# Another order of all steps up to the attention's end, in attention followed by two MLPs

## The chip, the cores and the metric

The kernel runs on one core of a Trainium2 chip. The metric is the device time of one launch in microseconds (us), and less is better. The kernel before took 616.63 us (median of 3 runs, 615.5 to 617.96).

## The reference

All inputs and outputs are float32. The attention takes `q`, `k`, `v` of shape (2, 8, 768, 64): 2 batches, 8 heads, 768 positions, 64 numbers per head. Each position attends to the positions less than 16 away and to 24 block summaries (the maximum of the keys, the mean of the values over 32 positions):

```python
k_sum = k.reshape(B, H, nb, block, D).max(axis=3)     # block = 32
v_sum = v.reshape(B, H, nb, block, D).mean(axis=3)
scores_l = scale * np.matmul(q, k.transpose(0, 1, 3, 2))   # masked outside the window
scores_s = scale * np.einsum('bhsd,bhnd->bhsn', q, k_sum) + np.log(block)
a = softmax(np.concatenate([scores_l, scores_s], axis=-1))
x = np.matmul(a, np.concatenate([v, v_sum], axis=2))       # then to 1536 tokens x 512
h = x @ w_in;  x = (h * (1 / (1 + np.exp(-h)))) @ w_out    # first MLP: 512 -> 2048 -> 512
out = ((x @ w_a) * (x @ w_b)) @ w_out2                     # second: 512 -> 1536 -> 512
```

## The kernel before

TensorE multiplies in a reduced float32 format (fp32r). To keep the precision, each operand of a large product is split into a high part, rounded to fp32r, and a low part, the rest; a product is then three matmuls (high by high, high by low, low by high).

The work has three stages. The first does the attention and, woven into it, the first MLP for tokens 0 to 895 or so; the second finishes the first MLP; the third is the second MLP. The change touches the first stage alone.

The attention goes in 24 steps, 12 per batch, each for 64 positions of all 8 heads. Ahead of a batch's steps the keys are brought into place and transposed on TensorE (`tk`), copied into window tiles (`wk`), and their block maxima taken (`mk`, joined by `sk`, put into the windows by `pk`); the values are loaded (`LG`), summed (`sv`), averaged by matmuls (`mv`) and kept (`kv`, copied on by the DMAs `PV`); the queries are transposed (`tq`) and scaled (`bq`). A step `n` then goes through scores (`sc`, TensorE, L403), masking with the row maximum (`sm`, VectorE, L427 or L433), exp (`ex`, ScalarE, L447), the sums (`rs`), the scaling (`no`, L462), a transpose (`tr`, TensorE, L468) and its copy out of PSUM (`pc`), the product with the values (`av`, TensorE, L483), and the split of the result into the high and low parts of the MLP's input x (`xh`, `xl`, L497).

The first MLP works on blocks of 512 tokens (8 attention steps) and pieces of 128 of the 2048 hidden units. For slot `i` (block `i // 16`, piece `i % 16`), `m1` makes the h tile with 12 matmuls (L579), `sg` applies Silu, `gh` and `gl` split it, and `m2` adds its share to the four y banks with 12 matmuls (L612). `m1` needs the piece of `w_in`, `m2` that of `w_out`, both loaded (`LI`, `LO`), decoded from raw words (`da` on ScalarE, `du` and `dj` on VectorE, L523, L529 and L533) and split (`hi`, `lo`, L556). A decoded `w_out` piece is also spilled to DRAM (`SP`) and read again for the later blocks (`RO`, `hR`, `lR`). The key, query, value and weight loads are all issued from SP's queue. Steps named `dm` with the letter y run four transposes on TensorE that keep it busy; with n they do nothing.

The order of all of this is one text, `ORDER` (L28 to L79): 797 words, carried out from left to right. Each word names a step, the numbers say which tile, and the last letter says which engine a movable step uses: `a` ScalarE, `v` VectorE, `p` GpSimd; for `sc` and `av` the last letter says whether a step opens new PSUM banks (n) or takes the second halves of those of the step before it (s). Each engine, and SP's queue, works through its own instructions in the order of the text, and an instruction that waits holds back everything behind it on its engine. Buffers are shared in small rings (four tiles of raw weight words, three decoded ones, three split `w_out` pieces, three g tiles, two h banks, four tiles of scores), and the next user of a ring waits for the release. After the last word a loop runs slots 28 to 47 with a fixed pattern, `m1` of a slot and then `m2` of the slot two before.

```python
        for word in ORDER.split():
            name, *a = word.split(":")
            ops[name](*(int(x) if x.isdigit() else x for x in a))
```

Of the kernel before, what the change touches and what calls it, by code (L numbers as in the profile page):

```python
# [32 lines left out]
sc:0:n sm:0 dm:8:n ex:1 rs:1 no:2:v LI:1 mv:0:1:0:1 mv:0:3:0:4 sv:0:2:1:p mv:0:2:0:1 kv:0:0:v LI:2 no:1:p ex:3 rs:3 ex:0 qz
tq:0:1:0 tq:0:1:1 bq:0:1:1:v tr:1 LV:1 pc:1:v du:in:2 du:in:1 dm:2:y bq:0:1:0:a sc:4:n sm:4 da:in:2 no:3:p da:in:1 tr:3
sc:5:n rs:0 no:0:p dj:in:2 sc:7:s dm:3:n tr:2 PV:0:1 LV:3 ex:4 av:1:n sm:7 PV:0:3 rs:4 LQ:0:2 tr:0 sm:5 hi:in:2:p pk:0:2:p
pc:3:a ex:7 xh:1:v pc:0:v av:3:n xh:3:v pc:2:a xl:1 LV:0 no:4:p sc:6:n lo:in:2:p dm:4:y rs:7 sm:6 xl:3 tq:0:2:0 no:7:p
tq:0:2:1 bq:0:2:1:v tr:4 ex:5 av:0:n xh:0:v ex:6 rs:6 dj:in:1 bq:0:2:0:a no:6:p PV:0:2 LV:2 av:2:n xh:2:a dm:9:n tr:7 xl:0
# [5 lines left out]
tr:8 pc:8:a tk:1:0:1 gh:2:a gl:2:p gh:0:a m1:4 mk:1:0:1 gl:0:v dj:in:7 hi:in:3:v lo:in:3:p tk:1:0:0 av:8:n LV:11 av:11:s
gh:1:a wk:1:0:1:a mk:1:0:0 LK:1:2 tk:1:2:1 wk:1:1:1:a hi:in:7:a xh:8:v xh:11:v tk:1:2:0 LQ:1:0 tq:1:0:0 tq:1:0:1 mk:1:2:1
wk:1:2:0:v mk:1:2:0 LI:6 sk:1:v wk:1:0:0:a tr:10 LO:1 gl:1:p xl:8 wk:1:2:1:a pk:1:0:v LV:9 lo:in:7:p xl:11 du:out:1 m1:3 tr:9
bq:1:0:1:a bq:1:0:0:a sc:15:n sc:13:s da:in:6 pc:10:a du:in:6 sg:3:p dj:in:6 sc:14:n sc:12:s da:out:1 dj:out:1 hi:in:6:a
lo:in:6:p LV:10 pc:9:a sm:15 hi:out:1:a lo:out:1:p sm:12 LO:0 LI:13 da:in:13 sm:13 av:10:n LI:5 SP:1 du:in:13 sg:4:p dj:in:13
av:9:s da:out:0 hi:in:13:a xh:9:a du:out:0 du:in:5 xh:10:a dj:out:0 sm:14 m1:6 sg:6:v xl:9 lo:in:13:p hi:out:0:a lo:out:0:v
da:in:5 LO:2 du:out:2 dj:in:5 da:out:2 dj:out:2 hi:in:5:v m1:7 boot LG:1:0 su:15:v LG:1:1 m2:0 ex:12 LQ:1:1 gh:6:v lo:in:5:v
m2:1 xl:10 hi:out:2:v lo:out:2:v gl:6:v LO:3 LI:8 da:out:3 du:out:3 SP:0 rs:12 dj:out:3 hi:out:3:v LG:1:2 tq:1:1:0 LG:1:3  # L50
tq:1:1:1 bq:1:1:0:a gh:3:a ex:14 SP:3 m2:2 da:in:8 bq:1:1:1:a gl:3:v sv:1:1:1:p sg:7:p lo:out:3:v m1:5 m2:3 no:12:v LO:5
sv:1:2:1:v mv:1:2:256:1 sv:1:0:1:v mv:1:0:256:1 pk:1:1:p mv:1:1:0:1 sv:1:3:1:v mv:1:3:0:1 LO:4 sg:5:v gh:5:a du:in:8 rs:14
no:14:p ex:15 kv:1:2:a gl:5:v LI:10 du:out:4 kv:1:0:a pk:1:2:a SP:2 dj:in:8 da:out:4 dj:out:4 LV:14 LV:12 hi:in:8:a lo:in:8:v
m1:13 hi:out:4:a tr:14 pc:14:a LI:9 lo:out:4:p gh:4:a du:out:5 tr:12 pc:12:v da:out:5 dj:out:5 hi:out:5:a su:13:v ex:13 m1:8
gl:4:v LO:7 rs:13 sc:18:n sc:16:s du:in:9 sm:16 sm:18 da:in:9 SP:4 LO:6 da:out:6 du:out:6 dj:in:9 PV:1:2 no:13:p rs:15 ex:18
m2:4 dj:out:6 LV:15 tr:13 LO:8 av:14:n av:12:s xh:12:v lo:out:5:p m2:5 sg:13:p xl:12 SP:5 xh:14:v hi:in:9:p LO:10 lo:in:9:p
no:15:v du:in:10 m1:9 pc:13:a LV:13 da:in:10 tr:15 du:out:8 hi:out:6:a lo:out:6:p xl:14 m2:6 sg:8:v gh:8:v da:out:8 gl:8:v
sg:9:v PV:1:3 SP:6 dj:in:10 du:out:7 gh:9:a PV:1:1 dj:out:8 pc:15:a hi:in:10:v da:out:7 dj:out:7 av:15:n LI:11 lo:in:10:v
av:13:n du:out:10 gh:7:a xh:13:v xl:13 xh:15:a xl:15 gl:9:v hi:out:7:a hi:out:8:v LI:15 lo:out:7:p m1:10 lo:out:8:v sc:17:n
gl:7:v sc:19:s LQ:1:2 du:in:11 sm:17 SP:8 m2:7 m2:8 ex:16 su:17:p LI:12 da:in:11 dj:in:11 hi:in:11:v sm:19 rs:16 SP:7  # L60
tq:1:2:1 ex:17 da:out:10 LO:9 tq:1:2:0 m1:16 du:in:12 da:in:12 dj:in:12 rs:17 no:17:v lo:in:11:p LI:14 sg:10:v hi:in:12:v
gh:10:a gl:10:v bq:1:2:0:a LV:18 du:out:9 da:out:9 lo:in:12:v bq:1:2:1:a dj:out:9 LO:11 m1:12 dj:out:10 hi:out:9:a SP:10
lo:out:9:p m2:9 da:in:14 rs:18 no:18:p du:in:14 dj:in:14 hi:in:14:v hi:out:10:a lo:out:10:v tr:18 lo:in:14:p LO:13 sg:16:p
du:out:11 LO:12 du:out:12 SP:9 da:out:11 dj:out:11 SP:11 tr:17 da:out:12 dj:out:12 m1:11 SP:12 sg:12:v LO:14 gh:12:v gl:12:v
sg:11:v gh:11:v m2:10 hi:out:11:a lo:out:11:p gl:11:v da:in:15 pc:18:v gh:13:v gl:13:p m1:22 da:out:13 m2:11 du:in:15
dj:in:15 LV:17 pc:17:v hi:out:12:p LV:16 no:16:v lo:out:12:v tr:16 av:17:n gh:16:a m1:14 du:out:14 LO:15 du:out:15 hi:in:15:p
sg:22:p lo:in:15:p da:out:14 m2:12 gl:16:v m1:17 dj:out:14 SP:14 hi:out:14:v da:out:15 dj:out:15 ex:19 du:out:13 dj:out:13
first xh:17:v SP:13 pc:16:v hi:out:13:v lo:out:13:v xl:17 sc:22:n sc:21:s sm:21 sg:14:p m2:13 gh:14:v gl:14:p m1:15 sm:22
sc:20:n lo:out:14:p m2:14 su:21:v sm:20 rs:19 ex:21 sg:15:v sg:17:p no:19:v su:22:p ex:22 tr:19 av:18:n gh:15:v hi:out:15:v
RO:18 lo:out:15:v LV:19 SP:15 gh:17:a av:16:s xh:18:a m1:18 rs:22 ex:20 rs:21 no:21:v RO:17 hR:17:a gl:15:v xh:16:a m2:15  # L70
yh:0:2 xl:18 xl:16 RO:16 yh:0:1 pc:19:v yh:0:0 sc:23:n hR:16:v lR:16:v yh:0:3 gl:17:p sm:23 m1:19 hR:18:p RO:25 lR:18:p
sg:18:p tr:21 gh:18:p gl:18:v m2:16 lR:17:p m2:17 m2:18 sg:19:p m1:21 RO:23 hR:23:v no:22:v LV:21 rs:20 no:20:v gh:19:p
gl:19:p m1:24 gh:22:v gl:22:p sg:21:p gh:21:p gl:21:v RO:19 lR:23:v tr:20 pc:21:a av:21:n av:19:s xh:19:a pc:20:a hR:19:v
sg:24:p ex:23 LV:23 rs:23 m1:20 sg:20:p xl:19 xh:21:a xl:21 RO:21 lR:19:p m2:19 gh:20:p RO:20 gl:20:v hR:20:v m1:25 m1:23
sg:23:p tr:22 lR:20:v m2:20 hR:21:p RO:27 hR:27:p lR:21:v m2:21 lR:27:p m1:27 gh:24:a gl:24:v RO:22 hR:22:a gh:23:v gl:23:v
RO:24 lR:22:p m2:22 no:23:p pc:22:v hR:24:p lR:24:p LV:22 m2:23 m2:24 tr:23 sg:25:v hR:25:v gh:25:v av:22:n gl:25:v m1:26
# [1083 lines left out]
```

## Time and profile before

| | |
|---|---|
| median of 3 runs | 616.63 us |
| the profiled execution | 617.56 us |
| its span, first to last instruction | 615.9 us |
| TensorE busy | 605.8 us of the span |
| VectorE, ScalarE, GpSimd busy | 397.7, 281.2, 279.3 us |
| TensorE's mean granted clock | 0.992 of full speed |

In the rows PE is TensorE's matmuls, PEld its weight loads, DVE VectorE, ACT ScalarE, POOL GpSimd, and SPq SP's queue; "L612" is a line of the kernel. The granted clock is given as a share of 2.4 GHz. Busy times of PE overlap from one matmul to the next, so a stop is seen from the starts and from the brackets, which give the idle time before an instruction and what ended it.

### The profile page before, as it was taken

To read this page: it belongs to the slowest core of one execution; us is meant where nothing else is said; L and a number is where in the kernel's file an instruction comes from. 1 tells how busy PE (TensorE), PEld (TensorE's weight loads), DVE (VectorE), ACT (ScalarE), POOL (GpSimd) and SP (SyncE) were. 2 spreads that over 40 slices of the span, in tenths; PEclk is the share of its full clock that TensorE was granted. 3 is DMA by queue.
4 is the path that set the end of the run, shared out by engine and by line. 5 is a ranking of instruction groups with operands and counts; after the bars stand their busy time and mean duration, and the time that the engine had idled before them with its cause. 6 is when DMAs were issued, how large, how long until landed. Compare 5 with 4: busy or idle time off the path is not lost.

```text
span 615.9 us, 10100 instructions
## 1 busy us (share of the span) xinstructions
PE 605.8 (98%) x3650; PEld 529.8 (86%) x3650; DVE 397.7 (65%) x778; ACT 281.2 (46%) x615; POOL 279.3 (45%) x269
## 2 busy tenths in 40 slices
...
PEclk9699999999999999999999999999999999999999
...
GB/s 222 191 240 232 252 315 227 259 232 105 44 56 79 78 86 218 221 227 173 200 192 171 48 52 147 128 208 135 144 186 96 195 35 87 82 219 315 120 0 137
DMA packets 90522, 97.82 MB, mean 159 GB/s; under 512 B 39000, under 2 KB 68440, under 8 KB 90472
## 3 DMA queue, kind: packets, MB, share of 16 engines
...
## 4 chain that ended last, share of the span: by engine, by line
PE 93%; DVE 3%; DMA 2%; issue 1%; ACT 0%; SPq 0%; DVEq 0%; ACTq 0%
PE y L612 21%; PE h L579 21%; PE bankg L823 14%; PE bankh L823 14%; PE ol L870 11%; PE o L849 5%; PE av L483 2%; PE sc L403 2%; PE pt L468 2%; DMA st_in<-in_moe_w_in_dram 1%; DMA st_k<-in_k_dram 1%; PE vsum L340 1%; PE qt L264 1%; PE kt L264 1%; DVE ks L302 1%
## 5 line engine op out<-in xcount | busy, mean ns | idle before, releaser
L612 PE MATMUL y<-g,w_out 128*128 128x512 f32 x576 | 139.1, 392 | 1.2 <-DVE st L433 1.0
L579 PE MATMUL h<-x,w_in 128*128 128x512 f32 (+1 forms) x600 | 139.9, 384 | 0.0
L612 PEld LDWEIGHTS y<-g,w_out 128*128 128x128 f32 x576 | 107.0, 188 | 25.3 <-ACT w_out L151 1.4
L579 PEld LDWEIGHTS h<-x,w_in 128*128 128x128 f32 x600 | 108.4, 188 | 21.8 <-DVE w_in L556 0.2
L556 POOL TENSOR_TENSOR w_out<-re_out,w_out 128x512 fp32r<-128x512 f32 x39 | 54.7, 1404 | 99.4 <-ACT w_out L151 95.0
L870 PE MATMUL ol<-w_out,plh 128*128 128x512 f32 x192 | 59.0, 389 | 0.0
L594 DVE TENSOR_TENSOR g<-h,g 128x512 fp32r<-128x512 f32 x31 | 21.4, 690 | 37.2 <-ACT g L151 36.9
L587 ACT ACTIVATE h<-h 128x512 f32<-128x512 f32 x31 | 18.2, 586 | 56.6 <-PE h L579 56.5
L556 POOL TENSOR_TENSOR w_out<-w_out,w_out 128x512 fp32r<-128x512 f32 x20 | 28.4, 1428 | 33.7 <-ACT w_out L151 26.4
L788 POOL TENSOR_TENSOR ab<-sum,ab 128x384 f32<-128x384 f32 x24 | 27.3, 1144 | 33.7 <-DVE sum L785 33.7
L870 PEld LDWEIGHTS ol<-w_out,plh 128*128 128x128 f32 x192 | 36.0, 188 | 7.5
L870 PE MATMUL ol<-w_out,pll 128*128 128x512 f32 x96 | 37.3, 389 | 0.0
L862 DVE TENSOR_TENSOR pll<-pl,plh 128x1024 fp32r<-128x1024 f32 x12 | 17.2, 1430 | 30.7 <-ACT plh L861 30.7
L151 ACT CAST w_out<-re_out 128x512 fp32r<-128x512 f32 x34 | 21.1, 621 | 27.9 <-issue 23.2
L849 PE MATMUL o<-w_out,p 128*128 128x512 f32 x108 | 28.5, 393 | 0.0
L823 PE MATMUL bankh<-yhT,wab 128*128 128x384 f32 x96 | 28.2, 334 | 0.0
L462 POOL TENSOR_TENSOR sm<-sm,st 128x480 f32<-128x480 f32 x14 | 15.3, 1095 | 27.6 <-DVE st L458 16.7
L533 DVE SCALAR_TENSOR_TENSOR w_out<-w_out,u_out 128x512 uint32<-128x512 uint32 x28 | 23.9, 860 | 4.2 <-ACT w_out L523 3.1
L766 ACT COPY sum<-bankh 128x384 f32<-128x384 f32 x12 | 5.7, 478 | 38.9 <-PE bankh L823 38.9
L594 POOL TENSOR_TENSOR g<-sg,g 128x512 fp32r<-128x512 f32 x8 | 10.7, 1343 | 27.8 <-ACT g L151 13.9
L523 ACT ACTIVATE w_out<-st_out 128x512 f32<-128x512 f32 x28 | 18.8, 674 | 9.5 <-DMA st_out<-in_moe_w_out_dram 5.1
L806 ACT CAST p<-ab 128x384 fp32r<-128x384 f32 x12 | 6.2, 514 | 35.5 <-POOL ab L788 18.0
...
## 6 DMA issues: line engine op xcount, KB each, us to landing
...
```

The source lines that it names most:

```text
L151: nc.scalar.copy(o, i)
L523: nc.scalar.activation(w32, stage_t[kind, f][:, :, 1].bitcast(F32), AF.Prelu, scale=2.0 ** -112, alpha=2.0 ** 32)
L533: nc.vector.scalar_tensor_tensor(bits, bits, 3, u_t.pop((kind, f)), op0=ALU.logical_shift_left, op1=ALU.bitwise_or)
L556: engine.tensor_tensor(w[:, 1], w32_t[kind, f], w[:, 0].bitcast(F32), op=ALU.subtract)
L579: nc.tensor.matmul(h_ps[i][:, cols], win_t[f][:, a, c * P:(c + 1) * P], x_t[n][:, steps, m, c, :], start=(idx == 0), stop=(idx == 3 * NK - 1))
L587: nc.scalar.activation(sg_t[i], ps, AF.Silu)
L594: engines[engine].tensor_tensor(g_t[i][:, 1], sg_t.pop(i), g_t[i][:, 0].bitcast(F32), op=ALU.subtract)
L612: nc.tensor.matmul(y_ps[n, c], wout_t[i][:, a, c * P:(c + 1) * P], g_t[i][:, m, :], start=(f == 0 and (a, m) == (0, 0)), stop=(f == N1 - 1 ...
L788: engines["v" if k == 6 else "p"].tensor_tensor(at, x, at, op=ALU.mult)
L823: nc.tensor.matmul((A, B)[b], weights(u, a, s, s + 1)[:, 0, c * P:(c + 1) * P], yc_t[q, y][m][:, c, :], start=(idx == 0 and not more), sto ...
L849: nc.tensor.matmul(o_ps[t], g[:, a, c:c + P], w[:, m], start=(begins and (a, m) == (0, 0)), stop=(ends and (a, m) == PARTS[-1]))
L870: nc.tensor.matmul(late_o[j], late_p[f][a][:, j * P:(j + 1) * P], wo2_t[N2 + f][:, m], start=(f == 0 and (a, m) == (0, 0)), stop=(f == N2 ...
```

## The change

The text of `ORDER` is replaced. The same 797 words stand in it, but in another order; for 132 of them the letter of the engine is another one, and 10 of the `sc` and `av` words and six `dm` words change their last letter (five `dm` words run in either order). No function of the kernel changes. The start of the two texts, to a little past the first `m1`:

```diff
-LKq:0:0 br:k:0:0:a dm:1:y tk:0:0:1 c2 LKq:0:2 ok:0 br:k:0:2:v tk:0:0:0 mk:0:0:0 tk:0:2:0 mk:0:2:0 wk:0:0:1:a c1 wk:0:0:0:a
-wk:0:2:0:a tk:0:2:1 LKq:0:1 br:k:0:1:v tk:0:1:1 tk:0:1:0 mk:0:2:1 dm:7:y LQq:0:0 dm:11:y wk:0:2:1:a mk:0:0:1 LG:0:1
-br:q:0:0:v tq:0:0:0 wk:0:1:0:a tq:0:0:1 mk:0:1:1 LG:0:0 mk:0:1:0 sk:0:v bq:0:0:0:a bq:0:0:1:a wk:0:1:1:v c3 pk:0:0:a sc:2:n
-sm:2 sc:1:n pk:0:1:a LG:0:2 sm:1 sv:0:1:1:p ex:2 sc:3:n sm:3 LG:0:3 LQ:0:1 rs:2 sv:0:3:4:v sv:0:0:4:p mv:0:0:512:4 dm:0:n
...
-sc:11:n sc:9:s dm:5:n LI:0 pc:4:a rs:5 hi:in:1:a no:5:p xl:2 pc:7:a sc:8:n ok:1 sc:10:s sm:11 tr:6 LV:7 sm:9 tr:5 LV:5 sm:10
-ex:11 av:7:n pc:6:a LV:4 av:4:n rs:11 xh:7:a xl:7 xh:4:a sm:8 dm:10:n pc:5:a lo:in:1:p LV:6 dm:6:n no:11:p m1:1:0 LK:1:1 ex:8
+c1 LKq:0:0 c3 dm:9:y LKq:0:1 br:k:0:1:a br:k:0:0:v tk:0:0:0 tk:0:0:1 ok:0 wk:0:0:1:a LKq:0:2 br:k:0:2:p mk:0:0:0 wk:0:0:0:a
+LQq:0:0 br:q:0:0:p tk:0:1:1 mk:0:1:1 wk:0:1:1:a qz LG:0:1 tk:0:1:0 wk:0:1:0:a mk:0:0:1 dm:4:n c2 tk:0:2:1 dm:11:y mk:0:2:1
+wk:0:2:1:a tk:0:2:0 mk:0:2:0 tq:0:0:0 bq:0:0:0:a mk:0:1:0 sk:0:v pk:0:0:p LG:0:3 wk:0:2:0:a tq:0:0:1 sv:0:3:4:p dm:10:y
+dm:5:n bq:0:0:1:v sc:2:n sm:2 ex:2 sc:1:n LG:0:0 sm:1 sv:0:1:1:p sc:3:n sm:3 ex:3 rs:2 no:2:v sv:0:0:4:p LQ:0:1 tq:0:1:0 rs:3
+ex:1 dm:6:y sc:0:s tq:0:1:1 dm:0:n sm:0 bq:0:1:1:v LG:0:2 sv:0:2:1:v pk:0:2:v bq:0:1:0:a mv:0:0:512:4 mv:0:1:0:1 mv:0:3:0:4
...
+xl:0 pc:7:v sc:11:n LI:0 da:in:0 sc:9:s sm:9 tr:6 LV:4 av:4:n sc:8:n sc:10:s LV:7 pc:6:a dm:8:n dm:3:n dm:1:y xh:4:v xl:4
+sm:11 ex:11 LV:6 av:6:s dj:in:2 sm:8 av:7:n LI:7 xh:7:a xl:7 tr:5 xh:6:v xl:6 hi:in:2:p m1:1:0 pc:5:a LV:5 av:5:s ex:9
+du:in:0 dj:in:0 rs:9 lo:in:2:p xh:5:a hi:in:0:p xl:5 sm:10 LK:1:0 tk:1:0:0 mk:1:0:0 ex:8 rs:8 su:10:v LI:4 da:in:4 ex:10
+LK:1:1 lo:in:0:p du:in:4 no:8:v dj:in:4 hi:in:4:p m1:2 sg:2:p LK:1:2 lo:in:4:p gh:2:a m1:1:1 sg:1:p gh:1:a tk:1:1:1 rs:10
...
```

## Rows read from the trace of the kernel before

**Rows 1.** The page's slices: TensorE's granted clock, in tenths of full speed, 40 slices.
```profile
PEclk9699999999999999999999999999999999999999
```

**Rows 2.** Stretches: busy us of each engine (instructions), granted clock, DMA share, GB/s.
```profile
6.30:16.40 10.10, 7.04 (x76) 5.73 (x76) 8.93 (x16) 7.36 (x25) 5.05 (x8) 1.00 1.12 249
16.50:26.70 10.20, 10.20 (x70) 9.38 (x70) 5.97 (x23) 6.94 (x33) 5.22 (x6) 0.50 0.80 183
26.80:40.40 13.60, 13.60 (x270) 11.38 (x268) 12.74 (x70) 11.43 (x48) 9.19 (x12) 1.00 1.01 209
40.40:72.30 31.90, 30.81 (x319) 26.82 (x316) 27.81 (x93) 26.95 (x70) 12.08 (x10) 1.00 1.03 260
72.30:223.20 150.90, 150.60 (x957) 122.05 (x958) 104.84 (x246) 78.55 (x162) 51.83 (x47) 1.00 0.53 151
```

**Rows 3.** The chain that ended last, in order of time: start us, us, what.
```profile
96.17 2.99 PE y L612 x12
...
329.33 8.16 PE y L612 x36
```

**Rows 4.** TensorE's timeline, 0 to 16 us: start, us, instruction, idle before it.
```profile
6.36 1.10 PE L264 MATMUL kt<-ident,raw_k 128*128 128x128 f32 x8 [0.40 <-ACT raw_k L151]
...
9.86 1.09 PE L264 MATMUL kt<-ident,raw_k 128*128 128x128 f32 x8 [0.95 <-DVE raw_k L153]
...
14.74 1.35 PE L403 MATMUL sc<-kin,qb 64*64 64x120 f32 x32 [1.60 <-ACT kin L151]
```

**Rows 5.** TensorE's timeline, 16 to 75 us.
```profile
20.86 2.92 PE L340 MATMUL vsum<-vg,sel 96*120 96x128 f32 x12
23.56 1.91 PE L264 MATMUL qt<-ident,raw_q 128*128 128x128 f32 x8
...
40.42 1.68 PE L579 MATMUL h<-x,w_in 128*128 128x256 f32 x12
...
65.62 5.75 PE L579 MATMUL h<-x,w_in 128*128 128x512 f32 x24
72.37 2.95 PE L612 MATMUL y<-g,w_out 128*128 128x512 f32 x10 [1.00 <-DVE st L433]
```

**Rows 6.** VectorE's timeline: copies of keys and queries, the joins, x.
```profile
7.07 0.69 DVE L153 COPY raw_k<-st_k 128x1024 f32<-128x1024 f32 x1 [3.90 <-DMA st_k<-in_k_dram]
...
11.00 0.69 DVE L153 COPY raw_q<-st_q 128x1024 f32<-128x1024 f32 x1
...
12.99 1.31 DVE L308 TENSOR_TENSOR ks<-ks 128x96 f32<-128x96 f32 x1
...
43.61 0.89 DVE L497 TENSOR_TENSOR x<-av,x 128x256 fp32r<-128x256 f32 x2 [0.29 <-ACT x L151]
...
59.93 0.26 DVE L308 TENSOR_TENSOR ks<-ks 128x96 f32<-128x96 f32 x1
```

**Rows 7.** ScalarE's timeline: the first copy, and the starts of two exps.
```profile
5.26 1.05 ACT L151 COPY raw_k<-st_k 128x1024 f32<-128x1024 f32 x1 [2.96 <-DMA st_k<-in_k_dram]
...
32.36 0.40 ACT L447 ACTIVATE sm<-sm,st 128x120 f32<-128x120 f32 x1
...
34.03 0.36 ACT L447 ACTIVATE sm<-sc,st 128x120 f32<-128x120 f32 x1
```

**Rows 8.** GpSimd's timeline: two copies.
```profile
30.25 0.61 POOL L153 CAST w_in<-w_in 128x512 fp32r<-128x512 f32 x1
30.80 0.34 POOL L153 COPY kin<-ks 128x192 f32<-128x192 f32 x1
```

**Rows 9.** Groups by shape, 0 to 224 us: count, busy us, mean ns, idle before.
```profile
L433 DVE CUSTOM_DVE_ANT_0 sm<-sc,mask 128x120 f32<-128x120 f32 x76 | 16.5, 277 | 8.0 <-PE sc L403 7.6 <-PE pt L468 0.2
...
L556 POOL TENSOR_TENSOR w_in<-w_in,w_in 128x512 fp32r<-128x512 f32 x10 | 13.5, 1352 | 8.9 <-ACT w_in L151 7.0 <-DVE w_in L153 1.3 <-DMA sp_out<-w_out 0.4
...
L587 ACT ACTIVATE sg<-h 128x512 f32<-128x512 f32 x17 | 10.2, 599 | 16.5 <-PE h L579 13.9 <-DVE g L594 2.6
...
L594 DVE TENSOR_TENSOR g<-h,g 128x512 fp32r<-128x512 f32 x11 | 7.5, 686 | 0.1
```

More of the change, by code (lines that the diff above doesn't have):

```diff
@@ L33 @@
[L33 to L37, printed above, removed]
@@ L38 @@
-sc:11:n sc:9:s dm:5:n LI:0 pc:4:a rs:5 hi:in:1:a no:5:p xl:2 pc:7:a sc:8:n ok:1 sc:10:s sm:11 tr:6 LV:7 sm:9 tr:5 LV:5 sm:10
-ex:11 av:7:n pc:6:a LV:4 av:4:n rs:11 xh:7:a xl:7 xh:4:a sm:8 dm:10:n pc:5:a lo:in:1:p LV:6 dm:6:n no:11:p m1:1:0 LK:1:1 ex:8
-su:10:v xl:4 du:in:0 tr:11 av:6:n LI:3 xh:6:a xl:6 av:5:n tk:1:1:0 xh:5:a da:in:0 tk:1:1:1 xl:5 m1:1:1 dj:in:0 ex:10
-hi:in:0:v lo:in:0:v rs:8 ex:9 rs:9 sg:1:p no:8:v no:9:p rs:10 LI:4 da:in:4 no:10:p mk:1:1:1 m1:2 sg:2:p m1:0:0 LI:7 LV:8
-m1:0:1 pc:11:a mk:1:1:0 wk:1:1:0:a du:in:4 dj:in:4 hi:in:4:v da:in:3 lo:in:4:v da:in:7 du:in:7 sg:0:v LK:1:0 du:in:3 dj:in:3
@@ L43 @@
[L43 to L76, printed above, removed]
@@ L77 @@
-sg:26:v pc:23:v LV:20 lR:25:v RO:26 hR:26:p lR:26:p av:20:s xh:20:v xl:20 gh:26:v av:23:n xh:23:a xl:23 RO:28 m2:25 sg:27:p
-xh:22:v gl:26:v xl:22 gh:27:a gl:27:p att
+c1 LKq:0:0 c3 dm:9:y LKq:0:1 br:k:0:1:a br:k:0:0:v tk:0:0:0 tk:0:0:1 ok:0 wk:0:0:1:a LKq:0:2 br:k:0:2:p mk:0:0:0 wk:0:0:0:a
+LQq:0:0 br:q:0:0:p tk:0:1:1 mk:0:1:1 wk:0:1:1:a qz LG:0:1 tk:0:1:0 wk:0:1:0:a mk:0:0:1 dm:4:n c2 tk:0:2:1 dm:11:y mk:0:2:1
+wk:0:2:1:a tk:0:2:0 mk:0:2:0 tq:0:0:0 bq:0:0:0:a mk:0:1:0 sk:0:v pk:0:0:p LG:0:3 wk:0:2:0:a tq:0:0:1 sv:0:3:4:p dm:10:y
@@ new lines @@
+dm:5:n bq:0:0:1:v sc:2:n sm:2 ex:2 sc:1:n LG:0:0 sm:1 sv:0:1:1:p sc:3:n sm:3 ex:3 rs:2 no:2:v sv:0:0:4:p LQ:0:1 tq:0:1:0 rs:3
+ex:1 dm:6:y sc:0:s tq:0:1:1 dm:0:n sm:0 bq:0:1:1:v LG:0:2 sv:0:2:1:v pk:0:2:v bq:0:1:0:a mv:0:0:512:4 mv:0:1:0:1 mv:0:3:0:4
+mv:0:2:0:1 rs:1 pk:0:1:a ex:0 rs:0 kv:0:0:a no:3:p tr:3 LV:0 pc:3:a sc:4:n no:1:v tr:1 LI:1 sm:4 da:in:1 LV:1 sc:5:n sc:7:s
+du:in:1 no:0:v tr:0 sm:7 LI:2 ex:4 dj:in:1 hi:in:1:p lo:in:1:p tr:2 sm:5 pc:1:a ex:7 LV:3 rs:4 da:in:2 sc:6:n sm:6 ex:6
+no:4:p PV:0:1 ex:5 av:1:n pc:2:v rs:7 PV:0:3 av:3:s LQ:0:2 tq:0:2:0 LV:2 pc:0:v no:7:p av:0:n xh:1:v xh:0:a xl:1 rs:6 no:6:v
@@ new lines @@
+tr:7 xh:3:v PV:0:2 xl:3 bq:0:2:0:a du:in:2 tq:0:2:1 rs:5 no:5:p ok:1 bq:0:2:1:a dm:2:n av:2:s xh:2:a xl:2 tr:4 pc:4:a dm:7:n
+xl:0 pc:7:v sc:11:n LI:0 da:in:0 sc:9:s sm:9 tr:6 LV:4 av:4:n sc:8:n sc:10:s LV:7 pc:6:a dm:8:n dm:3:n dm:1:y xh:4:v xl:4
+sm:11 ex:11 LV:6 av:6:s dj:in:2 sm:8 av:7:n LI:7 xh:7:a xl:7 tr:5 xh:6:v xl:6 hi:in:2:p m1:1:0 pc:5:a LV:5 av:5:s ex:9
+du:in:0 dj:in:0 rs:9 lo:in:2:p xh:5:a hi:in:0:p xl:5 sm:10 LK:1:0 tk:1:0:0 mk:1:0:0 ex:8 rs:8 su:10:v LI:4 da:in:4 ex:10
+LK:1:1 lo:in:0:p du:in:4 no:8:v dj:in:4 hi:in:4:p m1:2 sg:2:p LK:1:2 lo:in:4:p gh:2:a m1:1:1 sg:1:p gh:1:a tk:1:1:1 rs:10
@@ new lines @@
+no:10:p LI:3 LV:10 wk:1:0:0:v tk:1:1:0 mk:1:1:0 wk:1:1:0:a mk:1:1:1 gl:2:p tk:1:0:1 mk:1:0:1 wk:1:1:1:a tr:8 da:in:3 du:in:3
+gl:1:v da:in:7 tk:1:2:0 LI:6 dj:in:3 du:in:7 dj:in:7 hi:in:7:p wk:1:2:0:a tk:1:2:1 hi:in:3:a mk:1:2:1 lo:in:3:p wk:1:2:1:v
+m1:4 sg:4:p rs:11 m1:0:0 m1:0:1 LQ:1:0 pc:8:a m1:3 LO:0 mk:1:2:0 sk:1:v LO:1 no:11:v LV:8 sg:0:v lo:in:7:v da:in:6 tq:1:0:1
+gh:0:a wk:1:0:1:a du:in:6 tr:11 bq:1:0:1:a LV:11 da:out:1 LV:9 pc:11:v no:9:p sg:3:p tq:1:0:0 LI:13 bq:1:0:0:a tr:10 LG:1:2
@@ new lines @@
+tr:9 av:8:n du:out:1 pk:1:0:p dj:out:1 pc:10:a av:11:s sc:15:n sc:12:s du:out:0 dj:in:6 sc:13:n sc:14:s da:out:0 dj:out:0
+sm:12 sm:14 LI:5 gl:0:v xh:8:a hi:in:6:p hi:out:0:p lo:in:6:v pc:9:a av:9:n lo:out:0:p SP:0 sm:13 av:10:s xh:10:a xl:10 sm:15
+LO:2 pk:1:1:a xh:11:a xl:8 hi:out:1:a lo:out:1:p xl:11 m1:7 da:in:13 ex:14 LO:4 du:in:13 du:out:2 xh:9:a LQ:1:1 xl:9 ex:12
+dj:in:13 SP:1 da:out:2 m1:6 sg:6:v boot du:out:4 su:13:p dj:out:2 du:in:5 rs:12 hi:out:2:a lo:out:2:v m2:0 m2:1 LI:8
+sv:1:2:1:p hi:in:13:a lo:in:13:v tq:1:1:0 gh:4:a gl:4:v da:in:5 dj:in:5 hi:in:5:v lo:in:5:v tq:1:1:1 sg:7:p LO:3 da:out:3
@@ new lines @@
+m2:2 gh:6:a du:out:3 dj:out:3 m1:13 gl:6:v gh:3:a da:out:4 gl:3:v LG:1:0 SP:2 LI:9 bq:1:1:0:v hi:out:3:a dj:out:4 bq:1:1:1:a
+pk:1:2:a du:in:8 hi:out:4:a LG:1:3 sv:1:0:1:v m1:5 lo:out:3:v da:in:8 dj:in:8 hi:in:8:a LO:5 LG:1:1 lo:out:4:v du:in:9 m2:3
+m2:4 SP:3 lo:in:8:v sg:13:p SP:4 sv:1:1:1:v sg:5:v su:15:p ex:15 du:out:5 da:in:9 da:out:5 dj:out:5 hi:out:5:a mv:1:2:256:1
+sv:1:3:1:p mv:1:3:0:1 kv:1:2:v LI:12 LO:6 da:out:6 LI:10 mv:1:0:256:1 mv:1:1:0:1 no:12:v kv:1:0:a rs:14 gh:5:v gl:5:v m1:8
@@ new lines @@
+rs:15 LV:13 no:14:p LO:9 lo:out:5:p sg:8:v tr:12 du:out:6 dj:out:6 hi:out:6:v lo:out:6:p tr:14 pc:14:a pc:12:v dj:in:9 ex:13
+m2:5 SP:6 sc:18:n sc:16:s du:out:9 gh:8:a gl:8:v LV:14 sm:18 PV:1:3 m2:6 hi:in:9:a lo:in:9:v m1:9 da:in:10 sm:16 du:in:10
+LV:15 no:15:v dj:in:10 hi:in:10:v gh:7:p gl:7:p LO:7 ex:18 PV:1:1 lo:in:10:v tr:15 du:out:7 PV:1:2 av:14:n LV:12 av:12:s
+da:out:7 dj:out:7 rs:13 rs:18 hi:out:7:a ex:16 lo:out:7:p pc:15:a LO:8 da:out:8 m1:10 no:13:v xh:14:v du:out:8 dj:out:8
+du:in:12 SP:5 xl:14 sg:9:v gh:9:a tr:13 LI:14 SP:8 hi:out:8:v lo:out:8:p gl:9:v pc:13:v LO:11 da:out:9 dj:out:9 xh:12:v SP:7
@@ new lines @@
+SP:9 hi:out:9:p xl:12 no:18:p da:in:12 m2:7 m2:8 av:15:n sg:10:v gh:10:v gl:10:v da:out:11 av:13:n xh:13:v LO:10 du:out:11
+xh:15:v xl:15 lo:out:9:p m2:9 da:out:10 LI:11 dj:out:11 hi:out:11:a xl:13 m1:16 sc:17:n dj:in:12 hi:in:12:p du:in:14 sg:16:p
+lo:in:12:p sc:19:s LQ:1:2 gh:13:v gl:13:v du:out:10 dj:out:10 SP:10 da:in:11 du:in:11 dj:in:11 hi:in:11:v lo:in:11:v sm:17
+LO:12 LV:16 m1:17 sg:17:p su:17:v hi:out:10:v lo:out:10:v sm:19 rs:16 da:in:14 no:16:p SP:11 m1:11 dj:in:14 LO:13 sg:11:v
+da:out:13 gh:11:v gl:11:v m1:12 m2:10 LV:18 lo:out:11:p tq:1:2:1 hi:in:14:p lo:in:14:p ex:17 tq:1:2:0 rs:17 m2:11 LO:14
```

14 lines of the change are left out of this document (added).

## The prediction

> **What bounds the kernel now.** I read the slices of the page first: the clock granted to TensorE is full but near the start [rows 1]. Then the stretches: from 16.5 to 26.7 us the granted clock is 0.50 (1.2 GHz), on both sides of it 1.00 (2.4 GHz); in the stretch before the fall TensorE was busy 7.04 of 10.1 us, in short pieces [rows 2]. Then the chain that ended last: from about 82 us on TensorE is a metronome, 36 matmuls of 128x512 in 8.16 us, so 2.72 for twelve, and 2.99 where an attention step stands ahead of them [rows 3]. No order can shorten these, and the 393 us after the order's last instruction (223.2 us) hold the same work in both kernels.
>
> So what an order can win lies ahead of 82 us, and it is little. TensorE's own timeline shows its stops at the start: 0.40, 0.95 and 1.60 us, and a shorter one between the first two [rows 4]. The slow clock costs at most half of 10.2 us, 5.1; one sees it in eight transposes, 1.91 us long at 23.56 but 1.09 at 9.86 [rows 4, 5]. The last stop is ahead of the first y: 24 h matmuls start at 65.62, 5.44 us of work, and y starts at 72.37, 1.3 us late. The row names a VectorE reduction; its neighbour there, the low half of w_out 0, is what y lacks [rows 5]. Together that is some 10 us. What an order can lose has no such limit.
>
> **The change, part by part.** The order keeps its 797 steps. 132 of them change their engine: 61 leave VectorE and 56 come to it; GpSimd gets 44 and gives up 36, and what it gains are copies. Five keep-warm steps run in either order, and ScalarE changes between Exp and Silu 15 times in either: both nothing.
>
> *Start, to the first scores.* Now ScalarE brings key piece 0 (1.05), VectorE pieces 2 and 1 and the queries (0.69 each) [rows 6, 7]. In the new order VectorE brings piece 0, ScalarE piece 1, GpSimd piece 2 and the queries. Piece 0 lands as before, so its transposes start at 5.26 + 0.69 + 0.05 = 6.0 instead of 6.36. Piece 1 is now second in SP's queue, where VectorE's copy began at 7.07 [rows 6]: ready at 8.1. GpSimd's copy of 1024 elements stands in no row. Below it is bounded by VectorE's 0.69, above by two GpSimd tensor operations of 512 elements, 2.7 [rows 6, 9]. I take 1.03, the line through GpSimd's own copies of 192 (0.34) and 512 elements (0.61), its nearest rows [rows 8]. The queries were in by 11.00 [rows 6], so they are ready at 12.0 at the latest, and piece 2 ahead of them. Eight transposes (four take 0.43) end near 12.6, the maxima end by 13.0, and their join takes 0.26, its price when GpSimd rests, not the 1.31 it took beside GpSimd's sums [rows 6]. Then put_ksum on GpSimd (0.34) and the second query block on VectorE (0.69): first scores at 14.0 instead of 14.74, -0.7. With 2.7 for each copy it would be +2.0.
>
> *14 to 26 us.* The transposes of query tile 1 now come ahead of the value sums; the third value piece is loaded last and summed on VectorE. All this runs at the slow clock: four transposes 0.85, twelve sum matmuls 2.70 [rows 5]. The wait for query tile 1 (landing about 17.2 by its place in the queue) eats the 0.7. TensorE ends the sums at 25.8, having done as much as it now has at 25.3 plus 0.45: net 0.
>
> *26 to 46 us.* Here ScalarE and VectorE carry the time, busy 11.4 and 12.7 of 13.6 us [rows 2]. Both blocks of query tile 2 now stand on ScalarE behind exps 4, 7, 6 and 5 (1.6 each, 32.36 to 34.03 [rows 7]); before, one was on VectorE. My walk has them done at 36.3, and the first h matmul at 41.5, not 40.42 [rows 5]. Exp 11 waits for its masked scores, which on VectorE stand behind those of 9 (four of 0.28 and their reads [rows 9]) and two copies to x: 41.0, three us later than now. Behind it on ScalarE stand the copy of pt 5, exp 9 and the high part of x 5. So the last low part of x block 0, now done at 44.5 [rows 6], is done at 45.7. Every h but the first half of h 1 needs it. At 45.75, when h 2 starts, TensorE has 2.7 us less work behind it (half an h tile, three groups of four transposes) than at 45.97, when h 2 starts now: 2.5 us lost. Bounds: 0, if VectorE's idle time is as small as now (its program holds 121 instructions up to that point now, 116 then); 5, if ten of its operations with two SBUF inputs pay half of what the join paid.
>
> *46 to 82 us.* w_out 0 is loaded 1.1 MB earlier, and its low part, on GpSimd (1.35 [rows 9]), is ready at 67.8; the first y is wanted at 73.1. So the stop of 1.3 goes, and 0.7 at the next two y with it: -2.0. Late next are w_out 3 at its y, 88.6 for 87.7 (+0.9), and pt 9 (+0.3). w_in 3, moved back by 2.1 MB, lands near 52 us at 260 GB/s [rows 2]; its low part stands on GpSimd behind the high part of w_in 7 and is ready at 58.0, wanted at 58.3: nothing, but thin. Sum -0.8.
>
> *82 to 223 us.* The cover here is matmuls. Between the end of an h tile and its y lie at least 4.1 us of others (tiles 15 and 20; 5.6 now). The way is Silu 0.60, high part 0.61, low part 0.69 on VectorE or 1.35 on GpSimd [rows 8, 9]: 1.9 to 2.6, and 1.1 more where GpSimd holds VectorE up. Still covered; without cover each tile would pay that difference. SP's queue holds the same 119 issues; of those moved back, the vw load of step 8 is nearest to its use (62.4 for 63.9). Attention steps stand in 23 groups between big matmuls instead of 25, 0.27 each [rows 3]: -0.5.
>
> GpSimd holds VectorE up: the join took 1.31 beside a GpSimd sum and 0.26 alone [rows 6]. The Trainium skill, SBUF — State Buffer, "Who interferes with whom", says that a VectorE instruction with two SBUF inputs and a GpSimd one that reads SBUF exclude each other; the join's two rows agree. By that rule alone the copies added to GpSimd, some 4 us, speak against the change, up to +4 uncovered; past 72 us TensorE does not stop although VectorE is busy 105 of 151 us [rows 2], and so the trace puts it at nothing there.
>
> *Sum.* 0 + 0 + 2.5 - 0.8 - 0.5 = +1.2 us. The profiled execution took 617.56 us, its span 615.9 and 1.7 around it; it lies 0.9 above the median of 616.63. So 618.8 for such an execution, and 617.8 as a median.
>
> **Rivals.**
> *Faster: the clock does not fall.* TensorE gets its first scores 0.7 us earlier and is fed a little more ahead of 16.5 us. For it: 7.04 busy of 10.1 us brought the fall [rows 2], and a little more may not. Against it: three waits, on pieces 1 and 2 and the queries, lie in the same stretch. At the full clock the value sums would end with their last input, about 22.0, not 25.8: 3.8 less, and the 0.7 kept: 613.3. The Trainium skill, TensorE: Matmul & The Clock Gate, "What's actually happening", has the lower level as the default, which activity lifts; the stretch at 0.50 after short pieces agrees.
>
> *Slower: VectorE and GpSimd fall behind between 30 and 75 us.* The place is h 3, with 0.3 us of slack, behind low 2, high 7 and low 3 on GpSimd. If VectorE is more than that later than my walk, each us is TensorE's. Price: 1.5 more at the first whole h, 1.2 at h 3, 1.0 at the first y: +3.7, so 621.5. For it: the walk has no semaphore delays, and five of the first eight w_in high parts are on GpSimd. Against: the count of VectorE's instructions above.
>
> *It does nothing but move the waits about*, since buffers and amounts are the same: 616.6, inside the forecast's case.
>
> **How the numbers follow.** What can be told from no change is 0.5%, 3.1 us: 613.5 to 619.7. Forecast 617.8, own range 615.5 to 619.7, with the case of nothing: 0.50. Faster: 0.22. Slower: 0.28. The range for 8 in 10 reaches through both rivals, with the copies' upper bound of 2.0 on the slower one: 612.0 to 623.5.
>
> **What would show it.** Right: a granted clock of 0.50 from about 16.5 to 26.7; the first whole h near 45.8, behind x from VectorE; the first y near 73 without a stop; the metronome after 90 us; the order's end near 224.4. Wrong: no slow stretch, or a longer one; stops of TensorE over 1 us between 90 and 223 us; h 3 waiting for w_in; a 1024-element copy on GpSimd far from 1.03.

## The result, and the profile after

The changed kernel took 621.0 us (median of 18 runs, 614.52 to 622.98), the kernel before 614.79 us (median of 18 runs, 611.84 to 617.96). The ratio is 1.0077, 95% interval 1.0056 to 1.0098: 4.7 us slower, inside the range forecast (612.0 to 623.5), but beyond the +1.2 that was forecast.

The profiled execution took 621.82 us, its span is 620.0. First the slices of its page, TensorE's granted clock, to be read against [rows 1]; then the stretches of [rows 2], ending at after's own first h matmuls and first y, with the columns of [rows 2].

```profile
PEclk9999799999999999999999999999999999999999
```

```profile
6.30:16.40 10.10, 7.51 (x92) 6.14 (x92) 6.73 (x20) 8.10 (x28) 6.65 (x15) 1.00 1.17 260
16.50:26.70 10.20, 9.12 (x117) 7.70 (x118) 8.44 (x32) 9.29 (x42) 3.73 (x5) 1.00 0.99 218
26.80:41.50 14.70, 12.79 (x250) 10.66 (x248) 13.53 (x62) 11.89 (x48) 6.88 (x9) 1.00 0.93 212
41.50:73.00 31.50, 27.60 (x266) 23.73 (x262) 26.65 (x89) 22.99 (x56) 15.05 (x16) 0.89 1.09 270
73.00:225.00 152.00, 150.99 (x962) 122.86 (x961) 98.71 (x235) 77.74 (x158) 53.67 (x52) 1.00 0.50 144
...
67.80:73.10 5.30, 5.30 (x26) 4.32 (x26) 3.76 (x13) 4.13 (x10) 2.42 (x3) 0.50 0.83 209
```

The low clock has moved, in the slices from the second digit to the fifth: from 16.5 to 26.7 us it is 1.00 where before had 0.50, and the low level stands at 67.8 to 73.1 us instead, behind a stop. What comes ahead of it is in TensorE's timeline of after (start, us, instruction, idle before it), the counterpart of [rows 4, 5]:

```profile
13.97 1.05 PE L403 MATMUL sc<-kin,qb 64*64 64x120 f32 x32 [0.22 <-DVE qb L369]
...
16.67 0.63 PE L264 MATMUL qt<-ident,raw_q 128*128 128x128 f32 x4 [0.66 <-ACT sm L447]
...
30.43 0.69 PE L483 MATMUL av<-pts,vw 120*64 120x64 f32 x16 [0.97 <-DVE pts L153]
...
37.92 1.15 PE L483 MATMUL av<-pts,vw 120*64 120x64 f32 x32 [0.70 <-DMA vw<-in_v_dram]
39.00 0.65 PE L468 MATMUL pt<-ident,sm 128*120 128x128 f32 x4
39.41 1.68 PE L579 MATMUL h<-x,w_in 128*128 128x256 f32 x12
...
42.22 4.68 PE L579 MATMUL h<-x,w_in 128*128 128x512 f32 x24
...
63.28 0.69 PE L483 MATMUL av<-pts,vw 120*64 120x64 f32 x16
67.78 1.12 PE L483 MATMUL av<-pts,vw 120*64 120x64 f32 x16 [3.81 <-issue]
68.83 6.39 PE L579 MATMUL h<-x,w_in 128*128 128x512 f32 x18
...
92.57 3.69 PE L612 MATMUL y<-g,w_out 128*128 128x512 f32 x15 [1.01 <-DVE w_out L556]
```

The row to look at is the one at 67.78: TensorE stands for 3.81 us in front of the value product of step 10, and the releaser is "issue", which is idle time in which it waited for nothing that the profile names. With the half clock that follows (the 12 h matmuls behind it take 4.8 us for 2.72), the stop costs this execution some 6.5 us against full pace (4.0 at it, 0.5 in the product, 2.0 in the h tile), more than the whole loss.

What TensorE lacked shows in the page's DMA queues, which the prediction leaves out: queue q8, "instruction", moved 29 packets and 0.48 MB in all, so 16 KB each. TensorE's part of the trace has 7,397 rows (matmuls, weight loads and some that are not counted as busy), so that is a packet for every 256 instructions (q14's 21 packets of 8 KB are too few for that). These are the DMA rows (packets, MB, share) of 45.1 to 65.1 us, of before and then of after, and then of after from 65.1 to 66.5 us:

```profile
q1 hardware_dynamic: 11128, 4.95, 103.0%
q8 instruction: 2, 0.03, 0.7%
```

```profile
q1 hardware_dynamic: 9723, 5.30, 114.6%
q14 instruction: 1, 0.01, 0.1%
...
q1 hardware_dynamic: 251, 0.53, 100.9%
q8 instruction: 1, 0.02, 5.1%
q14 instruction: 1, 0.01, 1.6%
```

Before gets two of TensorE's packets in those 20 us; after gets none (its last had started at 44.99), then one at 65.22 us that ends at 66.36, and at 67.78 TensorE runs on. Counted from the start of the span, before has five by 65.1 us and after four. Where hardly a load is under way (148 to 208 us) they start at counts some 256 apart (2,460, 2,712 and 2,976 rows of TensorE done), and in none of the 13 profiles does one start less than 150 beyond a multiple of 256. So I take 150 beyond as the count at which a packet falls due, which is an estimate; in that stretch of after it starts 0.2 to 1.9 us later. The packet missing here fell due near 55 us by that count and came some 10 us later.

### The profile page after: what moved, and what is told of

It is laid out like the page before. It is cut to its first block, busy times and chain, and to the rows that moved or that the text cites. A ratio compares the mean times of both kernels' runs of the same rounds, so it can differ in the third digit from the quotient of the medians.

```text
span 620.0 us, 10097 instructions
## 1 busy us (share of the span) xinstructions
PE 603.4 (97%) x3650; PEld 527.1 (85%) x3650; DVE 395.3 (64%) x773; ACT 281.2 (45%) x612; POOL 282.0 (45%) x277
## 4 chain that ended last, share of the span: by engine, by line
PE 91%; DVE 3%; DMA 3%; SPq 1%; issue 1%; ACT 0%; POOL 0%; ACTq 0%; DVEq 0%
PE y L612 21%; PE h L579 21%; PE bankg L823 14%; PE bankh L823 14%; PE ol L870 11%; PE o L849 5%; PE av L483 2%; DMA vg<-in_v_dram 2%; PE pt L468 1%; PE sc L403 1%; DMA vw<-in_v_dram 1%; SPq L249 1%; PE qt L264 0%; PE kt L264 0%; DVE vg L326 0%
## 5 line engine op out<-in xcount | busy, mean ns | idle before, releaser
L579 PE MATMUL h<-x,w_in 128*128 128x512 f32 (+1 forms) x600 | 141.7, 388 | 0.0
L579 PEld LDWEIGHTS h<-x,w_in 128*128 128x128 f32 x600 | 109.9, 191 | 22.8 <-DVE x L497 0.3
L556 POOL TENSOR_TENSOR w_out<-re_out,w_out 128x512 fp32r<-128x512 f32 x38 | 52.8, 1388 | 112.3 <-ACT w_out L151 98.1
L556 POOL TENSOR_TENSOR w_out<-w_out,w_out 128x512 fp32r<-128x512 f32 x23 | 31.3, 1372 | 32.4 <-ACT w_out L151 26.4
L849 PEld LDWEIGHTS o<-w_out,p 128*128 128x128 f32 x108 | 19.9, 187 | 2.8
L700 POOL TENSOR_TENSOR wab<-c,wab 128x768 fp32r<-128x768 f32 x6 | 11.3, 1876 | 24.3 <-ACT wab L697 24.3
```

Of the source, the lines that this page charges most:

```text
L556: engine.tensor_tensor(w[:, 1], w32_t[kind, f], w[:, 0].bitcast(F32), op=ALU.subtract)
L579: nc.tensor.matmul(h_ps[i][:, cols], win_t[f][:, a, c * P:(c + 1) * P], x_t[n][:, steps, m, c, :], start=(idx == 0), stop=(idx == 3 * NK - 1))
L849: nc.tensor.matmul(o_ps[t], g[:, a, c:c + P], w[:, m], start=(begins and (a, m) == (0, 0)), stop=(ends and (a, m) == PARTS[-1]))
```

## The experiments

Theory 1: TensorE ran out of its own instructions, because their packet waited among loads. Theory 2: the value product of step 10 waited for its data. Beside them stands a question that the 18 runs of before raise, 611.8 to 618: is the half clock of its profile there in every execution?

**before_again** (no edit).

> The kernel before once more, to see its executions with their granted clock. If the half clock at 16.5 to 26.7 us is what separates its shorter executions (612) from its longer ones (616 to 618), the times fall into groups by clock: about 0.992 with 615 to 618, and 0.998 or more with 611.8 to 613.5, some 4 us apart. If the clock costs nothing because ScalarE, VectorE and the loads bound the start, clock and time are unrelated.

613.92 us (12 executions): four with a clock of 0.991 to 0.994 took 615.9 us and more, the eight at 0.999 or 1.0 took 614.7 and less. Profiled at 612.41 us, it held the clock. The stretch of [rows 2] at 16.5 us, and TensorE's first h and first y:

```profile
16.50:26.70 10.20, 8.98 (x132) 7.48 (x128) 8.54 (x33) 8.21 (x39) 6.14 (x7) 1.00 1.02 237
```

```profile
36.91 1.69 PE L577 MATMUL h<-x,w_in 128*128 128x256 f32 x12
...
61.77 5.73 PE L577 MATMUL h<-x,w_in 128*128 128x512 f32 x24
67.34 5.60 PE L610 MATMUL y<-g,w_out 128*128 128x512 f32 x24
```

The first h comes 3.5 us earlier than in [rows 5], and the stop ahead of the first y is not there. Over the 83 executions of before with a known clock, 54 held it (mean clock above 0.998): median 613.1 us. 28 did not (0.990 to 0.994): 616.0; one lay between. So the groups are 2.9 us apart, not the 4 expected; the two profiles, 5.15 us apart, stand near the ends of theirs. The three runs shown ahead of the prediction lay among the longer.

**before_warm**, to see what makes it fall:

```diff
-wk:0:2:0:a tk:0:2:1 LKq:0:1
+wk:0:2:0:a tk:0:2:1 dm:24:y dm:25:y LKq:0:1
...
-pk:0:0:a sc:2:n
+pk:0:0:a dm:20:y dm:21:y dm:22:y dm:23:y sc:2:n
```

> The order of before with six more keep-warm steps (24 transposes on TensorE) where it waits: two ahead of the third key piece, four ahead of the first scores. If TensorE's stops ahead of 16.5 us bring the fall of the clock, the granted clock stays at 1.00 in every execution and the median is 611.5 to 613.5, some 2 to 3 us under before. If the clock is not the price, or falls all the same: 614 to 617, or up to 1 us longer for the added transposes.

613.25 us (12 executions, 612.05 to 616.62), 0.999 of before [0.9971, 1.0009]. TensorE was busy 9.59 of the 10.1 us ahead of 16.4, and one execution in 12 had the low clock, where none was expected. That is fewer than 28 in 83, as if short stops there brought the fall, but 12 executions are too few to show it; the median, too, is not the 2 to 3 us under before that were expected, because most executions of before hold the clock anyway. The fall costs 2.9 us when it comes, by the two groups of before, and not the full half of 10.2 us: with the clock held TensorE waits for ScalarE in part of that time instead:

```profile
25.59 0.69 PE L481 MATMUL av<-pts,vw 120*64 120x64 f32 x16 [0.32 <-ACT sm L445]
26.72 0.65 PE L466 MATMUL pt<-ident,sm 128*120 128x128 f32 x4 [0.45 <-ACT pts L149]
```

**after_sc_later**: fewer instructions ahead of the late packet, the loads untouched.

```diff
-av:11:s sc:15:n sc:12:s du:out:0 dj:in:6 sc:13:n sc:14:s da:out:0 dj:out:0 sm:12 sm:14 LI:5 ... SP:0 sm:13 av:10:s xh:10:a xl:10 sm:15 ... m1:7
+av:11:s du:out:0 dj:in:6 da:out:0 dj:out:0 LI:5 ... SP:0 av:10:s xh:10:a xl:10 ... m1:7 sc:15:n sc:12:s sc:13:n sc:14:s sm:12 sm:14 sm:13 sm:15
```

> The order of after with the scores of steps 12 to 15 (64 matmuls with their 64 weight loads, 128 instructions of TensorE) and their maskings moved behind the h matmuls of slot 7; all loads stay where they are. Theory 1, TensorE stops from 63.96 to 67.78 us because its own next 256 instructions come late (the fetch starts at 65.22, 10 us after the point at which other fetches start): with 128 instructions fewer ahead of that point TensorE does not run out; no stop over 1 us between 60 and 70 us, no clock below 1.00 behind it, and a median of 614 to 616 instead of 621. Theory 2, the value product of step 10 waits for data (its values or its transposed weights): the stop stays in front of that product, until about 67.8, and the time at 620 to 623.

The stop at step 10 went, the time did not: 621.99 us (1.0133 [1.0102, 1.0164]). The edit made other waits: 1.47 us for a copy out of PSUM at 65.0, and this one ahead of the first y, behind which the clock fell too:

```profile
75.97 7.32 PE L609 MATMUL y<-g,w_out 128*128 128x512 f32 x24 [2.09 <-DVE x L494]
```

The place of the stop speaks for theory 1, and the time is a miss. It is weak evidence: in this profile the packet came at 61.4 us, so it was not late, and about half of the executions of after have no stop either (below).

**after_dma_later** and **after_two_later**: less load, TensorE's instructions untouched.

```diff
-LI:13 bq:1:0:0:a tr:10 LG:1:2 ... sm:14 LI:5 gl:0:v ... lo:out:0:p SP:0
+bq:1:0:0:a tr:10 ... sm:14 gl:0:v ... lo:out:0:p SP:0 LI:13 LG:1:2 LI:5
```

> The order of after with three loads moved later in SP's queue, from 55.3 to 59.5 us to behind the first spill (about 63.5 us): w_in 13, w_in 5 and a value piece of batch 1, 1.4 MB. TensorE's instructions stay where they are. Theory 1 (its instructions come late because the DMA engines are full of loads): the fetch that started at 65.22 starts by 62, the stop ahead of the value product of step 10 is under 1 us or gone, median 614 to 617. Theory 2 (that product waits for its own data, whose load was issued at 46.8 us, ahead of these three): stop and time as in after, 620 to 623.

The second leaves `LI:5` in its old place.

> The order of after with two loads (w_in 13 and a value piece of batch 1) behind the first spill, but w_in 5 left where it was, since moving it too made the h matmuls of slot 5 wait 1.6 us. Theory 1: fetch by 62 us, no stop at step 10's value product, and none at slot 5: 614.5 to 616.5. Theory 2: stop as in after, 620 to 623.

618.79 us (1.0087 [1.0060, 1.0114]) and 618.04 us (1.0070 [1.0048, 1.0091]). In both the packet comes at 61.8 and 60.7 us, there is no stop at step 10, and all 17 executions have a clock of 0.999 or more, where 15 in 29 of after have less. Yet the times are 1.5 to 1.8 us above the upper ends given. Loads are late where they are used: in the first profile slot 5 pays, in the row at 86.11 below. It names the split of a g tile, and that stood on VectorE behind the decoding of w_out 3, for whose load VectorE had waited 1.70 us (the last row); with w_in 5 in its old place, in the second, this stop is gone. There short stops are left, 0.53 and 0.65 us for w_out, and 0.43 for w_in 3, which stands ahead of the loads that were moved (after_again has 0.32 there with no edit). They add up to about half of what the second lies above the 615.0 of after without its stop; the rest I have not traced.

```profile
77.84 1.28 PE L261 MATMUL qt<-ident,raw_q 128*128 128x128 f32 x8 [0.94 <-DMA raw_q<-in_q_dram]
...
86.11 3.02 PE L576 MATMUL h<-x,w_in 128*128 128x512 f32 x12 [1.40 <-DVE g L591]
```

```profile
84.05 0.43 DVE L526 TENSOR_SCALAR u_out<-st_out 128x512 uint32<-128x512 uint32 x1 [1.70 <-DMA st_out<-in_moe_w_out_dram]
```

**after_more_warm**: the packets fall due earlier in the work, and all loads stay where they are.

```diff
-dm:4:n ... dm:5:n ... dm:0:n ... dm:2:n ... dm:7:n ... dm:8:n dm:3:n
+dm:4:y ... dm:5:y ... dm:0:y ... dm:2:y ... dm:7:y ... dm:8:y dm:3:y
```

> The order of after with its seven silent keep-warm steps switched on: 28 transposes and 28 weight loads more on TensorE, all ahead of 38 us, where it has 10 us of stops to put them in. Loads and all other steps stay. Theory 1 (TensorE's next 256 instructions come late): every fetch falls due 56 instructions earlier in the work, at the h matmuls some 6 us earlier, so the fetch that started at 65.22 us starts by 60 and TensorE does not run out; no stop at the value product of step 10, clock 1.00 there, median 614 to 616. Theory 2 (that product waits for data): the stop stays, 620 to 623.

616.1 us (12 executions, 615.01 to 617.86; 1.0034 [1.0014, 1.0053]). The packet comes at 54.2 us, no execution has a clock under 0.999, and TensorE never stops between 41.5 and 73 us:

```profile
41.50:73.00 31.50, 31.50 (x305) 27.45 (x304) 29.81 (x93) 27.66 (x78) 18.43 (x20) 1.00 1.05 271
```

28 transposes that compute nothing did away with the long executions; the median is 0.1 us above the upper end expected. Theory 2 has no reason for that.

**head_after** and **head_before**: one order up to the first h matmuls, the other for all that is left.

> The order of after up to its first h matmuls (182 words, to about 39 us), and from there the order of before for all that is left. If after's start loses 2 to 3 us to waits for ScalarE, VectorE and loads against a start of before in which the clock does not fall: clock 1.00 in nearly every execution, median 614.5 to 616.5, none under 613.5. If the loss of after lies behind 40 us alone: 612 to 613.5.

617.21 us (1.0038 [1.0017, 1.0059]). This is inconclusive: 2.18 us of it is a wait for step 11's scaling on GpSimd, just behind the seam, that neither order has. The clock held at the start.

> The order of before up to its first h matmuls (183 words, to about 40 us), and from there the order of after. If the late fetch near 60 us comes from after's loads between 50 and 60 us alone, executions with the stop and a lower clock (619 to 623) stay frequent. If it needs after's start too, they are rare, and the rest is before's time plus the 1.3 us of late w_out 3: 613.5 to 615.5, or 617 to 619 where the clock falls at 16.5 us.

620.33 us (1.0091 [1.0059, 1.0123]); the profiled execution stopped at step 10 for 3.17 us (its clock fell at 14.7 us too, for 3.4 us, so its time does not price the stop alone). So after's start is not needed for the stop; its loads and matmuls between 40 and 65 us are enough.

**after_again**, **after_again2** (no edit) and **after_two_warm** (only `dm:5` and `dm:3` switched on).

> The kernel after once more. Theory 1: its executions fall into two groups, without the stop (614.5 to 616.5, clock 0.999 or more) and with it (620 to 623, clock 0.997 or less); in a profile of the first group the fetch due at 54.8 us starts before TensorE has issued 1473 instructions, in one of the second it stops again at exactly that count.

> The same kernel a third time, for one more profile: as in the run before, a stop at 1473 instructions or none.

> The order of after with only two of its silent keep-warm steps switched on: 8 transposes, 16 instructions of TensorE. The fetch falls due 16 instructions, or 1.8 us of h matmuls, earlier. Theory 1: where the stop was 3.8 us it is about 2 us, at 1473 instructions again but 16 instructions earlier in the work, or gone; median 614.5 to 619. Theory 2: unchanged, 620 to 623.

These three decide between the theories. after_again took 616.23 us (614.28 to 623.1): six of its ten executions at 614.3 to 616.4 with clock 1.0, three at 620.5 and more, one at 617.1 between. The profile of one had the stop, after_again2 (614.67 us) had not. Its DMA rows from 60.3 to 61 us, and TensorE's timeline behind:

```profile
q1 hardware_dynamic: 376, 0.13, 126.2%
q8 instruction: 1, 0.02, 12.2%
```

```profile
63.98 1.15 PE L483 MATMUL av<-pts,vw 120*64 120x64 f32 x32
65.06 5.74 PE L579 MATMUL h<-x,w_in 128*128 128x512 f32 x24
70.64 4.70 PE L612 MATMUL y<-g,w_out 128*128 128x512 f32 x20
```

Same kernel, same loads, the packet at 60.4 us instead of 65.2, and no stop. And this is where TensorE stopped: its instructions up to 65.1 us in after, after_again, after_two_warm and, last, after_again2 (behind the stretch and its length: PE's busy us and count of matmuls, then PEld's and its count of weight loads):

```profile
0.00:65.10 65.10, 55.94 (x710) 47.90 (x711) 53.23 (x188) 49.91 (x163) 34.95 (x60) 1.00 1.03 238
```

```profile
0.00:65.10 65.10, 56.97 (x710) 48.61 (x711) 52.66 (x186) 49.98 (x163) 34.73 (x60) 1.00 1.03 235
```

```profile
0.00:65.10 65.10, 57.83 (x710) 49.69 (x711) 51.59 (x178) 49.62 (x163) 34.10 (x59) 1.00 1.00 232
```

```profile
0.00:65.10 65.10, 56.83 (x727) 48.90 (x727) 52.28 (x184) 50.01 (x163) 34.09 (x60) 1.00 1.00 234
```

Three executions of two orders stopped at the same count, 710 matmuls and 711 weight loads (head_before's shows 709 and 709; a record can be missing). By all rows of TensorE it is 1473 in each of the four, and in each TensorE starts again 1.3 to 1.4 us after the packet has ended. Yet in after_two_warm that count lies eight matmuls earlier in the work, in the middle of a product:

```profile
64.52 0.45 PE L483 MATMUL av<-pts,vw 120*64 120x64 f32 x8
69.02 1.55 PE L483 MATMUL av<-pts,vw 120*64 120x64 f32 x24 [4.05 <-issue]
```

A wait for data would have kept its place in the work; this one kept its count. after_two_warm missed the size that I gave it: 616.48 us (1.0075 [1.0042, 1.0107]), stopping about as often (five of its ten executions have a clock of 0.997 or less), and for longer in the profile. The packet does not start at a fixed time after it falls due; in the profiles made from after, but for after_more_warm, it got in at 60.4 to 61.8 us, or else not before 65.2 to 66.6.

## Why the prediction was right in its range and wrong in its working

That 621.0 lies inside the range, beside the 621.5 of the slower rival, is luck: neither that rival's mechanism nor the forecast's is what happened. Of the signs of being right, the low clock at 16.5 us, x as what the first whole h waits for, and the order's end did not come; of the signs of being wrong, the missing slow stretch did, and by a hair a stop of over 1 us behind 90 (1.01).

*The term that failed: the slow clock of before.* I took 16.5 to 26.7 us at 0.50 as a fixed cost of the kernel before, and forecast the same for after. It was one kind of execution. With the clock held (two executions in three) before takes 613.1 us; in all three profiles of after, and in those of its edits, it held there each time. The condition of the rival "the clock does not fall" came true, and its working of the place too: the value sums ended at 22.6 us for 22.0 forecast. Its price did not count against the median, since most executions of before don't pay it.

*Start.* Right: the first scores start at 13.97 us for 14.0 forecast, though so close by chance, since the other two profiles of after have 13.71 and 14.53. A 1024-element copy on GpSimd took 1.04 us for the 1.03 taken, and the join 0.26 beside a resting GpSimd:

```profile
8.81 1.04 POOL L153 COPY raw_k<-st_k 128x1024 f32<-128x1024 f32 x1 [1.41 <-DMA st_k<-in_k_dram]
...
10.91 1.04 POOL L153 COPY raw_q<-st_q 128x1024 f32<-128x1024 f32 x1 [1.06 <-DMA st_q<-in_q_dram]
```

```profile
12.80 0.26 DVE L308 TENSOR_TENSOR ks<-ks 128x96 f32<-128x96 f32 x1
```

*The loss up to h 2, +2.5.* Right in size against a before with its clock held, and wrong in its cause. h 2 starts at 42.42 us in after_again2 and at 42.48 in before_again, which has 2.7 us more work behind it by then: 2.6 lost. But no h waited for the last low part of x, so the size is luck: most of the loss is short stops from 15 to 38 us (0.66, 0.97 and 0.70 above). Between the first scores and h 2 TensorE is idle for 3.2 us in after_again2 and 1.6 in before_again.

*46 to 82 us, -0.8.* The stop ahead of the first y did go, and h 3 was not late in the first profile (0.32 us in after_again). But the gain was only there against the first profile of before: before_again and before_warm, with the clock held, have no such stop. I also misread it. The loads of w_out into TensorE show that y first lacked the high half of w_out 0, from ScalarE, and then for 0.58 us the low half, which I had named alone:

```profile
72.34 0.30 PEld L612 LDWEIGHTS y<-g,w_out 128*128 128x128 f32 x2 [1.39 <-ACT w_out L151]
73.21 0.77 PEld L612 LDWEIGHTS y<-g,w_out 128*128 128x128 f32 x4 [0.58 <-DVE w_out L556]
```

In after, w_out 3 came 1.01 us late at its y for the 0.9 forecast, though not in after_again2.

*82 to 223 us.* Right but for w_out 3: no other stop there is over 0.4 us. The order ends at 227.4 us where I forecast 224.4, and at 220.4 in after_again2, without the stop; that is 2.3 us behind before_again, as much as their times differ. The rival that VectorE and GpSimd fall behind did not happen.

*What no rival held.* I followed the engines and SP's queue and never asked how TensorE's own instructions arrive. Of the 29 executions of after, 15 have a clock below 0.998 and a median of 621.5 us, the other 14 one of 615.0. The first are taken here as those with the stop; the three profiles agree, the others show their clock alone. This adds up, as an estimate: 615.0 for 613.1 is +1.9 from the order's own waits; 15 in 29 times 6.5 is +3.4 from the stop; 28 in 83 times 2.9 is 1.0 that before pays for its own fall and after does not. Together +4.3, where the ratio gives 4.7.

The Trainium skill, Runtime: NRT & Kernel Launch, "Instruction fetch mechanics", says that an engine's program streams in by DMA, 256 instructions at a time, while the block before runs, and that the crossing is mostly hidden. The 16 KB packets agree; hidden it is in before, where TensorE never stops for it, and in the first profile of after it cost 3.81 us of standing still.

That the packet was late because of the loads is made likely by the two runs with loads moved, and not shown step by step. What stays open: which load a packet waits for, and why it gets in at 60.4 us in one execution and at 65.2 in another. And half of head_after's executions have a clock of 0.996 to 0.997 that its profile does not show.

The best of all that ran is before_warm, whose gain over before is too small to be told.
